# Which engine empties PSUM in three blocks of a weight gradient: the fourth quarter of `gw2`'s fifth to seventh block from VectorE to ScalarE

## The chip, the cores and the metric

The kernel runs on one core of a Trainium2 chip. Its time is the device time of one execution, in microseconds (us); the figure for a kernel is the median over its runs. A core has a matrix engine (TensorE, PE in the profile; its weight loads are PEld), a vector engine (VectorE, DVE), a scalar engine (ScalarE, ACT), GpSimd (POOL) and SyncE (SP). Each works through its own queue of instructions in order. In this kernel POOL and SP mainly start DMA transfers.

## The reference

Forward and backward pass of two residual blocks with layer norm in front, on one sequence of 2048 x 448 in bfloat16: a spectral filter (2-D real FFT, product with learned complex weights, inverse FFT), then an MLP over the sequence axis with 1792 hidden units.

```python
x = A_x
h  = x + irfft2(rfft2(layernorm(x)) * (w_r + 1j * w_i))
u  = gelu(einsum("bsd,sf->bdf", layernorm(h), w1) + b1)
h2 = h + transpose(einsum("bdf,fs->bds", u, w2) + b2)
# returned: h2, and the gradients of <h2, grad_out> to
# A_x, w_r, w_i, w1, b1, w2, b2
```

The gradient of `w2` (1792 x 2048, output 6) is the product of the hidden activations with `grad_out`, summed over the 448 channels. The gradient of `w1` (2048 x 1792, output 4) is built in the same way from the normed `h` and the gradient at the hidden units.

## The kernel before

The FFT is done as matmuls with tables: a 16-point part over the rows of a tile, a 128-point part and a 448-point part. `fft_rows`, `fft_cols` and `cmul` are the forward transform and the complex product; `ifft_cols` and `ifft_rows` the inverse. All of it is run twice, once forward and once for the gradient. The program is written in the order of the lines, but a scheduler places the instructions of independent parts between each other, engine by engine, by costs that it assumes; what comes out is a fixed order in each engine's queue. A tile pool gives out buffers in that order as they come free.

The change lies in the last third. There these pieces run side by side:

- `gw2(j, on)` (L657) makes block j of 14 of the gradient of `w2`, 128 rows by 2048. A block is made in four quarters of 512 columns. Each quarter is four matmuls (L662) that add up in one PSUM tile `ps_mm`, and one copy to the bfloat16 tile `s6` in SBUF. The letter `on[n]` says which engine copies quarter n: "a" ScalarE (L194), "v" VectorE (L196). When all four quarters are copied, POOL issues the store of the block (L172). Blocks count from 0; block 0 is called ahead of the transform, blocks 1 to 13 behind it in the text (L697), and the scheduler spreads them over the transform's work.
- `fft_cols` and `cmul` for the gradient: ScalarE copies `gi` (L346) and `ds` (L324), VectorE makes `gg` (L349) and the products (L362 to L365) on which the inverse waits.
- `ifft_cols` (L379, L380): matmuls; ScalarE copies `t1` (L396), VectorE adds and subtracts into `ab2` (L398, L400), and for two tiles the two engines copy one kind each to `ab2` (L194, L196).
- `ifft_rows`, once for each of 16 rows h: two matmuls L409 and two L411 that read `ab2`, ScalarE's copy `eo` (L194), then four matmuls L415 to L418 that read `eo`. Then `norm_back`: ScalarE's `v` (L612), VectorE's L615, L617 and L618, and the store of `gx`.
- the gradient of `w1` (L726 on): 16 blocks of four quarters (the fourth 256 wide), L732, all copied by ScalarE; in between `grad_w` (L712), whose load of `xs_b` needs the buffer that held `goT`.

PSUM has eight banks here in two pools: three buffers `ps_mm` (tag "mm"), which the quarters of `gw2` and of the `w1` gradient share, and five `ps_sp` (tag "sp") for the transform. `s6` has four buffers (tag "w4").

Of the kernel before, what the change touches and what calls it, by code (L numbers as in the profile page):

```python
# [113 lines left out]
def kernel(  # L114
# [32 lines left out]
    def w4(shape, name):  # L147
        return ring.tile(shape, BF16, tag="w4", bufs=4, name=name)
# [13 lines left out]
    def ps_mm(shape, dtype=F32):  # L162
        return psum.tile(shape, dtype, tag="mm", bufs=3, name="ps_mm")
# [7 lines left out]
    def st(out, in_, eng=None):  # L171
        return (eng or po).dma_start(out=out, in_=in_)  # L172
# [19 lines left out]
    def ev(out, in_, on):  # L192
        if on == "a":
            ac.copy(out=out, in_=in_)  # L194
        else:
            ve.tensor_copy(out=out, in_=in_)  # L196
# [460 lines left out]
    def gw2(j, on):  # L657
        s6 = w4([P, S], "s6")
        for n in range(4):
            pw = ps_mm([P, 512])  # L660
            for c in range(4):
                mm = pe.matmul(pw[:], lhsT=g_t[:, c, j * P:(j + 1) * P], rhs=goT[:, c, 512 * n:512 * n + 512],  # L662
                               start=(c == 0), stop=(c == 3))
            ev(s6[:, 512 * n:512 * n + 512], pw[:], on[n])
        first.append(mm)
        return st(out_6[j * P:(j + 1) * P, :], s6[:])
# [28 lines left out]
    st(out_7.rearrange("(q h) -> q h", h=NT), gb2b[:])  # L695

    for j in range(1, NFB):  # L697
        s6_st = gw2(j, "aaav")
        if j == 8:
            s6_mid = s6_st  # L700

# [69 lines left out]
```

## Time and profile before

| what | us |
|---|---|
| median of 3 runs (lowest, highest) | 372.22 (370.95, 372.51) |
| profiled execution | 371.55 |
| its span in the trace | 369.8 |
| TensorE busy in the span | 346.6 |
| VectorE busy | 236.3 |
| ScalarE busy | 217.4 |
| copies of `ps_mm` to `s` on ScalarE (L194) | 107, 57.5 busy |
| copies of `ps_mm` to `s` on VectorE (L196) | 13, 0.69 each |
| TensorE stopped for ScalarE's copies of `ps_mm`, 232 to 369 | 1.5 in 3 waits |

Busy time is the sum of the instructions' lengths in the trace. A matmul's length has the pipeline's fill in it, so two that follow each other without a gap start 0.216 us apart although each is 0.38 long; the text counts from start to start. A few matmul records are missing from a trace, so a group that is printed as x3 can be four. "Idle before" in a row is time in which the engine stood still ahead of the first of the group, with the instruction that ended it.

### The profile page before, as it was taken

What the parts mean: (1) busy time and instruction counts of PE and PEld (TensorE: products, weight loads), DVE (VectorE), ACT (ScalarE), POOL (GpSimd) and SP (SyncE); (2) the same over time, 40 slices, a digit from 0 to 9 for tenths busy, and PEclk for the clock granted to TensorE, in tenths of its full rate; (3) what the DMA queues carried; (4) which work ended last, traced back from release to release, by engine and by line L of the source; (5) the groups of instructions that cost most, each with busy time, mean ns of one, the idle gap of its engine ahead of it and who ended that gap; (6) DMA issues with size and microseconds to landing.
All of it is one profiled execution on the core that took longest, in us unless ns stands there. A gap on an engine that the chain in (4) does not pass through costs nothing.

```text
span 369.8 us, 5755 instructions
## 1 busy us (share of the span) xinstructions
PE 346.6 (94%) x2100; PEld 200.4 (54%) x2115; DVE 236.3 (64%) x557; ACT 217.4 (59%) x415; POOL 61.2 (17%) x107
## 2 busy tenths in 40 slices
PE   0698999999989999999999999999999999999996
PEld 0355667666645555555555555566655555665553
DVE  4873679967744999621167778468996566599000
ACT  2776555446659998109222234967656666777664
POOL 1000000001112211500540000101012522255311
PEclk9999999999999999999999999999999999999999
DMA  7999998997889999999998875791874444956633
GB/s 279 258 257 307 270 274 245 310 240 259 249 251 176 338 346 291 380 401 215 261 224 159 185 147 208 162 182 61 204 199 184 163 177 166 337 187 255 250 150 149
DMA packets 132524, 86.48 MB, mean 234 GB/s; under 512 B 91952, under 2 KB 123824, under 8 KB 131984
## 3 DMA queue, kind: packets, MB, share of 16 engines
q1 hardware_dynamic: 124304, 55.78, 61.2%
q0 software_dynamic: 8048, 30.31, 22.3%
q8 instruction: 16, 0.26, 0.3%
q14 instruction: 12, 0.10, 0.1%
q10 hardware_dynamic: 144, 0.03, 0.0%
HBM read 32.81 MB, written 30.76 MB: 172 GB/s over the span
## 4 chain that ended last, share of the span: by engine, by line
PE 65%; DVE 17%; ACT 8%; DMA 4%; SPq 3%; issue 2%; ACTq 0%; DVEq 0%
PE ps_mm L732 12%; PE ps_mm L662 10%; PE ps_sp L587 7%; PE ps_mm L438 6%; PE ps_mm L519 6%; PE ps_sp L519 5%; PE ps_mm L587 4%; DMA w2T<-in_B_w_dram 4%; DVE junk L615 3%; DVE junk L617 3%; ACT v L610 3%; SPq L175 2%; DVE t_r L362 2%; DVE gg L349 2%; DVE t_i L363 2%
## 5 line engine op out<-in xcount | busy, mean ns | idle before, releaser
L194 ACT CAST s<-ps_mm 128x512 bf16<-128x512 f32 (+1 forms) x107 | 57.5, 557 | 25.6 <-PE ps_mm L662 11.1
L662 PE MATMUL ps_mm<-goT,g_t 128*128 128x512 bf16 x214 | 53.3, 379 | 2.0 <-ACT s L194 1.5
L438 PE MATMUL ps_mm<-go_nat,w2T 128*128 128x448 bf16 x224 | 50.5, 357 | 1.0 <-DMA w2T<-in_B_w_dram 1.0
L732 PE MATMUL ps_mm<-du_t,hlnT 128*128 128x512 bf16 (+1 forms) x251 | 49.3, 352 | 0.3
L643 PE MATMUL ps_mm<-du,w1T 128*128 128x449 bf16 x224 | 43.4, 353 | 0.0
L732 PEld LDWEIGHTS <-hlnT 128*128 128x128 bf16 x256 | 25.1, 98 | 22.2
L587 PE MATMUL ps_sp<-gT,w2c 128*128 128x448 bf16 x140 | 35.6, 352 | 0.0
L610 ACT ACTIVATE v<-ps_mm,nm,rstd_h 128x448 f32<-128x448 f32 x16 | 11.6, 723 | 39.2 <-DVE nm L608 39.2
L172 POOL DMA_DIRECT2D out_dram<-s x29 | 15.6, 539 | 112.4 <-ACT s L194 86.3
L519 PEld LDWEIGHTS <-w1c 128*128 128x128 bf16 x224 | 21.8, 98 | 20.7 <-issue 1.9
L587 PEld LDWEIGHTS <-w2c 128*128 128x128 bf16 x224 | 21.9, 98 | 20.5
L643 PEld LDWEIGHTS <-w1T 128*128 128x128 bf16 x224 | 21.7, 97 | 20.7
L662 PEld LDWEIGHTS <-g_t 128*128 128x128 bf16 x224 | 21.6, 97 | 20.7 <-issue 1.4
L438 PEld LDWEIGHTS <-w2T 128*128 128x128 bf16 x224 | 21.9, 99 | 16.2 <-DMA w2T<-in_B_w_dram 1.9
L349 DVE TENSOR_TENSOR gg<-ps_sp,gi 128x450 bf16<-128x450 f32 x28 | 16.2, 621 | 17.0 <-ACT gi L346 17.0
L587 PE MATMUL ps_mm<-gT,w2c 128*128 128x448 bf16 x84 | 25.0, 352 | 0.0
L519 PE MATMUL ps_mm<-hln,w1c 128*128 128x448 bf16 x112 | 24.4, 352 | 0.5 <-DVE b1col L508 0.2
L194 ACT CAST eo<-ps_sp 128x450 bf16<-128x450 f32 x32 | 17.2, 538 | 12.5 <-PE ps_sp L411 12.2
L519 PE MATMUL ps_sp<-hln,w1c 128*128 128x448 bf16 x112 | 23.1, 352 | 0.0
L311 PE MATMUL ps_sp<-kf,eo 128*128 128x128 bf16 x128 | 9.3, 231 | 14.0 <-DVE eo L305 14.0
L592 DVE SCALAR_TENSOR_TENSOR h<-ps_sp,b2col,hr 128x448 bf16<-128x448 f32 x10 | 6.3, 679 | 25.1 <-PE ps_sp L587 25.1
L615 DVE CUSTOM_DVE_ANT_0 junk<-ps_sp,xr,rneg_x 128x448 bf16<-128x448 f32 x16 | 10.9, 683 | 16.3 <-ACT v L612 16.3
(146 smaller groups left out, 625.9 us busy)
## 6 DMA issues: line engine op xcount, KB each, us to landing
w1c<-in_B_w_dram SPq DMA_DIRECT2D x7, 1024.0 KB, 7.4
w2c<-in_B_w_dram SPq DMA_DIRECT2D x8, 896.0 KB, 12.6
out_dram<-s POOLq DMA_DIRECT2D x14, 512.0 KB, 2.9
out_dram<-s POOLq DMA_DIRECT2D x15, 448.0 KB, 2.9
xs_d<-xs SPq DMA_DIRECT2D x1, 1800.0 KB, 7.7
xs_b<-xs_d SPq DMA_DIRECT2D x1, 1800.0 KB, 8.9
x<-in_A_x_dram SPq DMA_DIRECT2D x4, 448.0 KB, 4.3
go_nat<-in_grad_out_dram SPq DMA_DIRECT2D x2, 896.0 KB, 7.5
```

The lines of the kernel that those rows point to most:

```text
L172: return (eng or po).dma_start(out=out, in_=in_)
L194: ac.copy(out=out, in_=in_)
L349: ve.tensor_tensor(out=gg[:], in0=pr[:], in1=gi[:], op=op)
L438: pe.matmul(pg[:], lhsT=w2T[j][:, t, :], rhs=go_nat[:, t, :], start=(t == 0), stop=(t == NT - 1))
L519: pe.matmul(pu[:], lhsT=wc[:, h, o:o + P], rhs=hln[:, h, :], start=(h == 0), stop=(h == NT - 1))
L587: pe.matmul(p2[i][:], lhsT=w2c[t0 // 4][:, j, i * P:(i + 1) * P], rhs=gT[:, j, :], start=(j == 0), stop=(j == NFB - 1))
L610: ac.activation(out=v[:], in_=ps[:, 0:D], func=ACT.Identity, scale=rstd_c, bias=nm1[:])
L615: ve.tensor_tensor_reduce(out=junk[:], in0=ps[:, 0:D], in1=xhat, scale=rneg_c, scalar=0.0, op0=ALU.mult, op1=ALU.add, accum_out=nm2[:])
L617: ve.scalar_tensor_tensor(out=junk[:], in0=xhat, scalar=nm2[:], in1=v[:], op0=ALU.mult, op1=ALU.add)
L643: w1_last = pe.matmul(pd[:], lhsT=w1T[:, j, :], rhs=du[:, j, 0:D + 1], start=(j == 0), stop=(j == NFB - 1))
L662: mm = pe.matmul(pw[:], lhsT=g_t[:, c, j * P:(j + 1) * P], rhs=goT[:, c, 512 * n:512 * n + 512], start=(c == 0), stop=(c == 3))
L732: pe.matmul(pw[:, 0:wdt], lhsT=hlnT[:, c, h * P:(h + 1) * P], rhs=du_t[:, c, 512 * n:512 * n + wdt], start=(c == 0), stop=(c == 3))
```

## The change

The call of `gw2` for blocks 4, 5 and 6 gets the string "aaaa" in place of "aaav". ScalarE copies the fourth quarter of these three blocks, VectorE no longer does. All other blocks keep "aaav". Nothing of the arithmetic is changed.

```diff
     for j in range(1, NFB):
-        s6_st = gw2(j, "aaav")
+        s6_st = gw2(j, "aaaa" if 4 <= j <= 6 else "aaav")
         if j == 8:
             s6_mid = s6_st
```

The scheduler's order changes with it. On ScalarE the copy of block 4's fourth quarter stands right behind that of the third quarter, ahead of two L324 copies; block 5's stands between the two `ab2` copies; block 6's behind the first row's `eo`. On TensorE the order is the same up to the first quarters of block 6. There, ahead of the first L415, six more matmuls of `gw2` are placed, and every later row of `ifft_rows` has the blocks of `gw2` and of the `w1` gradient six matmuls further on. On VectorE three copies are gone and the later copies of a fourth quarter move by a place or two against L617 and L618. On POOL the store of block 4 stands ahead of the first three loads of `xr` instead of behind them, and some later stores change places with the stores of `gx`. SP's order is the same.

## The prediction

> **What bounds the kernel now.** I read the page's busy shares and chain of waits first. TensorE is busy 94% and holds 65% of the chain, so a microsecond is won only where TensorE stands still. Then I read the windows over the stretch where `gw2` runs beside the inverse transform.
>
> ```profile
> PE 346.6 (94%) x2100; PEld 200.4 (54%) x2115; DVE 236.3 (64%) x557; ACT 217.4 (59%) x415; POOL 61.2 (17%) x107
> PE 65%; DVE 17%; ACT 8%; DMA 4%; SPq 3%; issue 2%; ACTq 0%; DVEq 0%
> ...
> 262.50:274.50 12.00, 11.64 (x86) 8.33 (x86) 12.00 (x23) 7.11 (x14) 1.63 (x3) 1.00 1.06 239
> 274.50:280.10 5.60, 4.20 (x26) 2.35 (x26) 4.05 (x8) 2.81 (x6) 1.08 (x2) 1.00 0.24 97
> 280.10:334.40 54.30, 53.68 (x315) 31.06 (x319) 37.43 (x81) 38.24 (x72) 19.32 (x34) 1.00 0.58 212
> 334.40:369.80 35.40, 31.80 (x168) 16.47 (x169) 7.34 (x16) 22.19 (x44) 10.19 (x19) 1.00 0.51 196
> ```
>
> The columns are window, length, then busy us (and instructions) of TensorE, its weight loads, VectorE, ScalarE, GpSimd. VectorE is full from 262.5 to 274.5 (12.00 of 12.00) while ScalarE works 7.11. From 274.5 to 280.1 TensorE loses 1.40 of 5.60; later it loses little, and the clock is 1.00 throughout. The timeline of TensorE, VectorE and ScalarE in that hole:
>
> ```profile
> 274.73 0.81 PE L662 MATMUL ps_mm<-goT,g_t 128*128 128x512 bf16 x3
> 276.21 0.81 PE L662 MATMUL ps_mm<-goT,g_t 128*128 128x512 bf16 x3 [0.67 <-ACT s L194]
> 276.86 0.36 PE L409 MATMUL ps_sp<-di,ab 128*128 128x225 bf16 x2
> 277.06 0.38 PE L662 MATMUL ps_mm<-goT,g_t 128*128 128x512 bf16 x1
> 278.11 0.38 PE L662 MATMUL ps_mm<-goT,g_t 128*128 128x512 bf16 x1 [0.67 <-ACT s L194]
> ...
> 280.08 2.97 PE L662 MATMUL ps_mm<-goT,g_t 128*128 128x512 bf16 x13
> 283.08 0.26 PE L415 MATMUL ps_sp<-eo,kinv 128*128 128x225 bf16 x1
> ...
> 276.60 0.76 DVE L196 CAST ab<-ps_sp 128x256 bf16<-128x256 f32 x2
> 277.26 1.29 DVE L196 CAST s<-ps_mm 128x512 bf16<-128x512 f32 x2
> ...
> 261.91 0.59 ACT L194 CAST s<-ps_mm 128x512 bf16<-128x512 f32 x1
> 263.51 1.13 ACT L324 CAST ds<-ps_sp 128x450 bf16<-128x450 f32 x2 [1.01 <-PE ps_sp L323]
> 275.58 0.58 ACT L194 CAST s<-ps_mm 128x512 bf16<-128x512 f32 x1 [0.49 <-PE ps_mm L662]
> 277.47 0.59 ACT L194 CAST s<-ps_mm 128x512 bf16<-128x512 f32 x1 [1.31 <-PE ps_mm L662]
> 278.71 0.54 ACT L194 CAST eo<-ps_sp 128x450 bf16<-128x450 f32 x1 [0.66 <-PE ps_sp L411]
> 282.49 0.54 ACT L194 CAST eo<-ps_sp 128x450 bf16<-128x450 f32 x1
> ```
>
> Call the quarter tiles by block and quarter: j4q4 is the fourth of the fifth block. The VectorE row at 277.26 is j4q4 and j5q4 together. The matmuls of j4q4 were over by 262.7 and those of j5q4 by 274.1, so two of the three `ps_mm` buffers sit full, behind VectorE's complex products and `ab` work. Blocks j6q1, q2 and q3 then share the one buffer that ScalarE empties: TensorE stops until the copy of j6q1 (275.58 to 276.16) and again until that of j6q2 (277.47 to 278.06).
>
> **The change, part by part.** *Removed:* three VectorE copies of 128x512, each 0.69 (0.60 from start to start), two at 277.26 and one at 281.21. Alone that is worth nothing, since VectorE's next work waits for ScalarE's `v` anyway. *Added:* the same three copies on ScalarE, 0.58 long and 0.48 from start to start.
>
> j4q4. Its matmuls end about 262.5 (the seven that start at 261.24, four of them its own), and a ScalarE copy starts 0.2 after the last matmul's slot (277.06 + 0.22 + 0.2 = 277.47, the row above), so it runs 262.7 to 263.3. That is inside the 1.01 of idle before 263.51. Queued behind it are the two L324 copies at 263.51, for which the full VectorE waits; they keep 0.2 of slack. Cost 0; without that cover it would be up to 0.58, on VectorE first.
>
> j5q4. It now stands between the two `ab` copies of 274.06 and 274.72: 274.43 to 274.95. The second `ab` copy ends about 275.3 instead of 275.1, before the copy of 275.58, and VectorE reaches the same tile only at 276.98. Cost 0.
>
> j6q4. It stands behind an `eo` copy in the queue, below.
>
> *Moved.* With the buffers free the order of the built program has TensorE doing six more matmuls of `gw2` before the first L415, and all later rows shift by six. POOL's queue gets the store of block j4 ahead of its three `xr` loads instead of behind. The store can issue at 263.3 and takes about 0.54, and POOL's first `xr` load goes at 267.25 because of TensorE and VectorE; cost 0. If it slipped, the first L615 (280.61) would still be more than 4 us behind the third `xr` load's landing (about 270.4 + 5.4). SP's queue is the same.
>
> *The hole.* A 512-wide matmul takes 0.216 from start to start (the 13 at 280.08: 2.97 less one length of 0.38, over 12). In the trace the next matmul could start at 275.38 and starts at 276.21, then 277.28 and 278.11: 2 x 0.83 = 1.67 lost (the printed 0.67 counts from the modelled end). In the changed order, from 275.38: j6q2 to 276.24; two of j6q3 to 276.67 (its buffer is j5q4's, empty at 275.0); the two L409 to 276.87 (`ab`'s first kind is done at 276.1); two of j6q3 to 277.30; three of j6q4 to 277.95 (buffer of j6q1, empty at 276.16); the two L411 to 278.15 (`ab` is done at 277.36); one of j6q4 and two of j7q1 to 278.79. `eo` follows L411's start by 0.39 (278.32 to 278.71) and L415 follows `eo` by 0.59 (278.71 to 279.30), so L415 starts at 277.95 + 0.98 = 278.92, against 279.30. That is 0.38 earlier with six matmuls more behind it, 0.38 + 6 x 0.216 = 1.67: all of the hole.
>
> *The rows.* From there on each row h is one L415 to L418, L409 and L411 (0.79, from 279.30 to 280.08) and then n matmuls of 512, while ScalarE empties quarters and then copies `eo`. L415 waits for `eo`: from the last matmul of the quarter emptied just ahead of it, 0.2 + 0.48 + 0.59 = 1.27. If k matmuls are queued after that quarter, the row loses 1.27 - 0.216k: 0.19 for k = 5, nothing for k = 6. The trace agrees: 280.08 + 13 x 0.216 = 282.88, and L415 comes at 283.08, `eo` at 282.49. Counting k in both orders: before, k is 5 in rows 1, 3, 4 and 8 (4 x 0.19), two rows of `grad w1` lose 0.25 each where a 256-wide quarter stands ahead, and one 0.03: 1.3. After, k is 5 in rows 1, 5, 9, 14 and 15 and row 12 loses 0.05: 1.0. Gain 0.3. Counted through, the last L415 starts at 278.92 + 15 x 0.79 + 179 x 0.216 + 2.2 (five sets of four 256-wide matmuls) + 1.0 = 332.5 against 334.02 in the trace, with two matmuls more behind it: 1.5 + 0.4 = 1.9. (The same count on the old order gives 334.0.)
>
> Behind the last row there are only matmuls back to back (31.80 busy of 35.40, the rest the tail), and ScalarE's 22.19 fits beside them, so the 1.9 arrives at the end. What VectorE is late with, the `grad_w` products that wait for `xs_b`, moves along: its load goes when the last `gw2` matmul has read `goT`, here about 311.1 instead of 312.9.
>
> [...]
>
> **Sum.** 1.67 + 0.3, or 1.9 by the count through. The profiled execution takes 371.55 (span 369.8 and 1.75 around it), so 369.65; the median shown is 372.22, 0.67 above it, so 370.3.
>
> **Rivals.** *More is won (gain 3.0).* If no row waited for `eo` after the shift, the 1.0 left goes too: 372.22 - 3.0 = 369.2. For it: k = 5 misses by only 0.19. Against: five rows have that k.
>
> *The hole becomes a wait for `ab` (gain 1.5).* L411 needs VectorE's last `ab` piece. The trace has it done at 277.36, 0.58 ahead, but a view of waits puts 1.0 of the weight loads' idling at L411 down to VectorE's copies at 277.26. If L411 cannot start before 278.32, as now, 0.38 is given back: 370.7.
>
> *Slower: ScalarE becomes the pacer of the rows.* Its queue is strict, `v` and two or three copies stand ahead of each `eo`, and the shift could leave one copy more there than I count: 0.48 in each of 15 rows, 7.2 - 1.9 = 5.3, so 377.5. It decides from 0.13 a row (the gain is gone) and from 0.25 a row it is slower by more than the line. For it: a row with three copies ahead already loses 0.25 (317.86). Against: ScalarE is busy 38.24 of 54.30, and the formula fits all rows of before within 0.05.
>
> **How the numbers follow.** The line between change and none is 0.5%, 1.86 us. Forecast 0.60, own range 369.8 to 370.8; its middle lies just past the line (370.36), and since VectorE's freed 1.8 is counted at nothing I put 0.36 of it past and 0.24 short. More won 0.12, faster. `ab` 0.10, same. ScalarE as pacer 0.18, of which 0.14 slower and 0.04 same. So faster 0.48, same 0.38, slower 0.14. The bounds of the unknown costs are row waits of nothing (369.2) and of 0.13 a row (372.2); with the spread of the runs, 369.0 to 372.5.
>
> **What would show it.** Right: no TensorE gap ended by a ScalarE copy between 274 and 279, first L415 near 278.9 after six more matmuls, the last near 332.5, and a ScalarE copy near 262.7 with L324 still at 263.5. Wrong: L324 later than 263.6, L411 waiting for VectorE, or rows whose L415 comes over 0.2 after the last matmul's slot.

## The result and the profile after

The changed kernel takes 370.37 us, the median of 13 runs (369.15 to 371.92); the kernel before, run beside it, takes 371.81 (13 runs, 370.95 to 373.69). The ratio is 0.9954 with a 95% interval of 0.9937 to 0.9971, so the change takes off 1.7 us (1.1 to 2.3); the two medians alone differ by 1.44. An unchanged time (a ratio of 1) lies outside the interval, the 0.5% line inside it. The profiled execution takes 369.54 and its span is 367.8, against 371.55 and 369.8.

This execution starts the first matmul of the gradient's inverse transform (L379) at 263.77, the one of before at 263.91. I therefore compare distances from that instruction. From it to the first L415 the kernel before needs 15.39 us and the changed one 15.03, with six more matmuls done in between; to the end of the span 105.89 and 104.03, which is 1.86 less. The span is printed to 0.1, so a distance to the end is good to some 0.05.

The page's busy shares and chain of waits, and the same four windows as before, with their ends moved to where this execution's stages end (length, then busy us and instructions of TensorE, weight loads, VectorE, ScalarE, GpSimd, then the clock, the DMA share and GB/s):

```profile
PE 347.4 (94%) x2115; PEld 200.6 (55%) x2115; DVE 234.6 (64%) x554; ACT 218.8 (60%) x418; POOL 61.2 (17%) x107
PE 67%; DVE 18%; ACT 8%; DMA 4%; issue 2%; ACTq 0%; DVEq 0%
...
262.50:274.50 12.00, 11.86 (x88) 8.35 (x86) 12.00 (x23) 7.91 (x15) 2.15 (x4) 1.00 1.19 240
274.50:280.10 5.60, 5.60 (x34) 3.10 (x32) 2.71 (x6) 3.97 (x8) 1.09 (x2) 1.00 0.95 231
280.10:332.90 52.80, 52.55 (x315) 30.49 (x314) 37.45 (x81) 38.08 (x72) 18.79 (x33) 1.00 0.57 207
332.90:367.80 34.90, 31.45 (x168) 16.17 (x166) 6.72 (x15) 21.79 (x43) 10.19 (x19) 1.00 0.50 194
```

The second window is the hole. TensorE is busy 5.60 of 5.60 there, where it was 4.20. VectorE lost three copies (557 instructions to 554) and is as full as before in the first window, 12.00 of 12.00; ScalarE got three (415 to 418). The timeline of TensorE, ScalarE and VectorE in the same stretch:

```profile
274.38 2.32 PE L662 MATMUL ps_mm<-goT,g_t 128*128 128x512 bf16 x10
276.54 0.36 PE L409 MATMUL ps_sp<-di,ab 128*128 128x225 bf16 x2
276.74 1.24 PE L662 MATMUL ps_mm<-goT,g_t 128*128 128x512 bf16 x5
277.82 0.36 PE L411 MATMUL ps_sp<-di,ab 128*128 128x225 bf16 x2
278.02 0.81 PE L662 MATMUL ps_mm<-goT,g_t 128*128 128x512 bf16 x3
278.80 0.26 PE L415 MATMUL ps_sp<-eo,kinv 128*128 128x225 bf16 x1
...
279.58 2.54 PE L662 MATMUL ps_mm<-goT,g_t 128*128 128x512 bf16 x11
282.15 0.26 PE L415 MATMUL ps_sp<-eo,kinv 128*128 128x225 bf16 x1
...
262.60 0.59 ACT L194 CAST s<-ps_mm 128x512 bf16<-128x512 f32 x1 [0.23 <-PE ps_mm L662]
263.37 1.14 ACT L324 CAST ds<-ps_sp 128x450 bf16<-128x450 f32 x2 [0.19 <-PE ps_sp L323]
...
274.19 0.59 ACT L194 CAST s<-ps_mm 128x512 bf16<-128x512 f32 x1
278.21 0.54 ACT L194 CAST eo<-ps_sp 128x450 bf16<-128x450 f32 x1 [0.26 <-PE ps_sp L411]
...
276.46 0.76 DVE L196 CAST ab<-ps_sp 128x256 bf16<-128x256 f32 x2
```

Neither of the two rows that ended in "[0.67 <-ACT s L194]" is left: ten matmuls run on without a stop, and the groups between L409, L411 and L415 follow at once. The two copies that freed the buffers are ScalarE's rows at 262.60 (fifth block) and 274.19 (sixth block). The first fills idle time: L324 has 0.19 of idle ahead of it where it had 1.01, and still starts when its own input comes. The view of what TensorE waited for, in the last third, has the `ps_mm` copies of ScalarE at 0.2 in one wait, after 1.5 in three.

### The profile page after: what moved, and what is told of

It reads as the page before. It is cut to its first block, busy times and chain, and to the rows that moved or that the text cites. A ratio compares the mean times of both kernels' runs of the same rounds, so it can differ in the third digit from the quotient of the medians.

```text
span 367.8 us, 5768 instructions
## 1 busy us (share of the span) xinstructions
PE 347.4 (94%) x2115; PEld 200.6 (55%) x2115; DVE 234.6 (64%) x554; ACT 218.8 (60%) x418; POOL 61.2 (17%) x107
## 4 chain that ended last, share of the span: by engine, by line
PE 67%; DVE 18%; ACT 8%; DMA 4%; issue 2%; ACTq 0%; DVEq 0%
PE ps_mm L732 12%; PE ps_mm L662 10%; PE ps_sp L587 7%; PE ps_mm L438 7%; PE ps_mm L519 6%; PE ps_sp L519 5%; PE ps_mm L587 4%; DVE junk L615 3%; DVE junk L617 3%; ACT v L610 3%; DMA w2T<-in_B_w_dram 3%; DVE t_r L362 2%; DVE gg L349 2%; DVE t_i L363 2%; PE ps_sp L321 2%
## 5 line engine op out<-in xcount | busy, mean ns | idle before, releaser
L194 ACT CAST s<-ps_mm 128x512 bf16<-128x512 f32 x110 | 59.5, 559 | 23.8 <-PE ps_mm L662 8.0
L662 PE MATMUL ps_mm<-goT,g_t 128*128 128x512 bf16 x224 | 54.8, 379 | 0.2 <-ACT s L194 0.2
L194 ACT CAST eo<-ps_sp 128x450 bf16<-128x450 f32 x32 | 17.2, 537 | 12.4 <-PE ps_sp L411 12.2
L615 DVE CUSTOM_DVE_ANT_0 junk<-ps_sp,xr,rneg_x 128x448 bf16<-128x448 f32 x16 | 10.9, 682 | 16.3 <-ACT v L612 16.3
```

What stands on the lines that cost most here:

```text
L615: ve.tensor_tensor_reduce(out=junk[:], in0=ps[:, 0:D], in1=xhat, scale=rneg_c, scalar=0.0, op0=ALU.mult, op1=ALU.add, accum_out=nm2[:])
```

## The experiments

All were compared with the kernel before on the same chip: its median was 372.14 (31 runs) beside the four kernels `e_block4`, `e_block5`, `e_block6` and `e_block4up`, and 372.24 (32 runs) beside the other four. "To the end" is the distance from the first L379 of the gradient to the end of the span: 105.89 before, 104.03 with the change.

### The fifth block's copy alone (e_block4)

```diff
-        s6_st = gw2(j, "aaav")
+        s6_st = gw2(j, "aaaa" if j == 4 else "aaav")
```

> Only block 4's fourth quarter on ScalarE. Buffers (my theory): one of the two stuck ps_mm buffers is enough to close the hole, since two buffers in turn keep TensorE fed (j6q3 reuses j6q1's, empty 0.1 us before it is wanted). TensorE's order is that of the full change, so the span falls by the full 1.9 us, no TensorE gap between 274.5 and 280. Rival, relief of VectorE or count of copies moved: a third of it, 0.6 us.

370.27 (8 runs), ratio 0.9943 (0.9923 to 0.9963). First L415 after 15.03, to the end 104.04: both are those of the whole change, within 0.01. TensorE and VectorE in the timeline:

```profile
275.98 2.32 PE L662 MATMUL ps_mm<-goT,g_t 128*128 128x512 bf16 x10
278.13 0.36 PE L409 MATMUL ps_sp<-di,ab 128*128 128x225 bf16 x2
...
278.06 0.74 DVE L196 CAST ab<-ps_sp 128x256 bf16<-128x256 f32 x2
278.73 0.67 DVE L196 CAST s<-ps_mm 128x512 bf16<-128x512 f32 x1
```

The sixth block's quarter is still held until VectorE's copy at 278.73. TensorE does its ten matmuls all the same, ending 0.6 before that copy starts, with the two buffers that are left.

### The sixth block's copy alone (e_block5)

```diff
+        s6_st = gw2(j, "aaaa" if j == 5 else "aaav")
```

> Only block 5's fourth quarter on ScalarE. Buffers: the same full 1.9 us, by the other stuck buffer. Rival, relief of VectorE: 0.6 us. If each copy had a share of its own, blocks 4 and 5 alone would add up to the whole; by my theory each alone is the whole.

369.98 (12 runs), ratio 0.9947 (0.9927 to 0.9966); first L415 after 15.03, to the end 103.99. Now it is the fifth block's quarter that stays behind VectorE, to 280.77, and again the stops are gone (TensorE and VectorE in the timeline):

```profile
278.02 2.32 PE L662 MATMUL ps_mm<-goT,g_t 128*128 128x512 bf16 x10
...
280.77 0.68 DVE L196 CAST s<-ps_mm 128x512 bf16<-128x512 f32 x1
```

The gains of the parts do not add: each of the two copies brings all of it alone. One buffer more is enough, and it does not matter which.

### The seventh block's copy alone (e_block6)

```diff
+        s6_st = gw2(j, "aaaa" if j == 6 else "aaav")
```

> Only block 6's fourth quarter on ScalarE. Buffers: both buffers stay stuck, TensorE keeps both stops of 0.83 us between 275 and 279, and the rows lose 1.15 against 1.3 us: gain 0.1 us, no change. Rival, relief of VectorE: 0.6 us faster.

371.88 (12 runs), ratio 0.9987 (0.9969 to 1.0005); first L415 after 15.39 as before, to the end 105.76, 0.13 less. TensorE's stops stay where they were:

```profile
276.35 0.81 PE L662 MATMUL ps_mm<-goT,g_t 128*128 128x512 bf16 x3 [0.67 <-ACT s L194]
276.99 0.36 PE L409 MATMUL ps_sp<-di,ab 128*128 128x225 bf16 x2
277.19 0.38 PE L662 MATMUL ps_mm<-goT,g_t 128*128 128x512 bf16 x1
278.24 0.38 PE L662 MATMUL ps_mm<-goT,g_t 128*128 128x512 bf16 x1 [0.67 <-ACT s L194]
```

This copy comes after the hole, and taking it from VectorE is worth next to nothing. So the third part of the change does not matter.

### Half of each held copy taken from VectorE, the buffers still held (e_split)

```diff
-            ev(s6[:, 512 * n:512 * n + 512], pw[:], on[n])
+            if j in (4, 5) and n == 3:
+                ev(s6[:, 1536:1792], pw[:, 0:256], "v")
+                ev(s6[:, 1792:2048], pw[:, 256:512], "a")
+            else:
+                ev(s6[:, 512 * n:512 * n + 512], pw[:], on[n])
```

> The fourth quarter of blocks 4 and 5 is halved: VectorE copies columns 0 to 255, ScalarE 256 to 511. VectorE is relieved by half and ScalarE takes over half, but both ps_mm buffers are still held until VectorE comes to its half behind the ab work. Buffers: TensorE keeps both stops between 275 and 279 (first matmul of the inverse to first L415 15.4 us, as before), gain at most 0.3 us, from the rows. Rival, relief of VectorE: about a third of the full gain or more, 0.6 us, with the stops shorter.

372.03 (12 runs), ratio 0.9993 (0.9969 to 1.0018); first L415 after 15.39, to the end 105.85. VectorE's two copies at the end of its backlog shrank from one row of 1.29 to this one of 0.76:

```profile
277.03 0.76 DVE L196 CAST ab<-ps_sp 128x256 bf16<-128x256 f32 x2
277.69 0.76 DVE L196 CAST s<-ps_mm 128x256 bf16<-128x256 f32 x2
```

TensorE nevertheless stops for 0.67 twice (until 276.65 and until 278.55). Both stops end with ScalarE's copy of the quarter before (276.02 and 277.91), as in the kernel before. So neither split tile was free for it: their halves start at 277.69 on VectorE and at 279.58 on ScalarE. Less work for VectorE, with the buffers held at least as long, is worth nothing. In the built order ScalarE's halves stand even later, behind `eo` (279.15), so this is a test of VectorE's load and not of splitting a tile at its best.

### Two more quarters behind VectorE (e_two_more_held)

```diff
+        s6_st = gw2(j, "aavv" if 4 <= j <= 5 else "aaav")
```

> Blocks 4 and 5 give their third quarter to VectorE too (aavv). Buffers: block 4 alone now holds two of three buffers from 262 to 277, so TensorE can place 15 matmuls of gw2 fewer ahead of the first L415 (93 against 108): 3.2 us of idle, of which 0.9 comes back because L415 starts earlier and 0.3 to 0.6 in the rows; about 1.8 us slower than before. Rival, engine time: VectorE has 1.2 us more behind its ab work, where it waits for v for 2.1 us anyway, so no change.

375.46 (7 runs), ratio 1.0082 (1.0054 to 1.0111): 3.0 more, where 1.8 was expected; to the end 109.52, 3.63 more. TensorE's rows:

```profile
276.42 0.36 PE L409 MATMUL ps_sp<-di,ab 128*128 128x225 bf16 x2 [1.21 <-DVE ab L398]
277.59 0.37 PE L411 MATMUL ps_sp<-di,ab 128*128 128x225 bf16 x2 [0.81 <-DVE ab L196]
278.18 0.38 PE L662 MATMUL ps_mm<-goT,g_t 128*128 128x512 bf16 x1 [0.22 <-DVE s L196]
...
279.79 4.21 PE L662 MATMUL ps_mm<-goT,g_t 128*128 128x512 bf16 x13
283.83 0.26 PE L415 MATMUL ps_sp<-eo,kinv 128*128 128x225 bf16 x1
```

With the buffers held by VectorE, TensorE has nothing left to do but the transform and waits for VectorE itself. The thirteen matmuls at 279.79 took 4.21; in the kernel before thirteen took 2.97. The windows of this kernel say why; the third figure from the end is the granted clock:

```profile
276.00:278.70 2.70, 1.23 (x7) 0.56 (x8) 2.70 (x7) 0.53 (x1) 0.00 (x0) 1.00 0.00 0
278.70:279.70 1.00, 1.00 (x8) 0.85 (x7) 0.62 (x2) 0.37 (x1) 0.41 (x1) 0.59 0.08 16
279.70:280.70 1.00, 1.00 (x5) 0.41 (x4) 0.69 (x2) 0.26 (x1) 0.13 (x1) 0.50 0.29 119
280.70:281.70 1.00, 1.00 (x4) 0.39 (x3) 0.39 (x1) 0.00 (x0) 0.00 (x0) 0.50 0.97 377
281.70:282.70 1.00, 1.00 (x4) 0.35 (x3) 0.96 (x3) 0.00 (x0) 0.13 (x1) 0.71 0.07 25
282.70:283.70 1.00, 1.00 (x7) 0.47 (x5) 0.32 (x1) 0.96 (x3) 0.80 (x2) 1.00 0.06 25
```

With the mixed windows (0.59 and 0.71) split between 0.50 and 1.00, the clock is at half for an estimated 0.82 + 1 + 1 + 0.58 = 3.4 us. The first row of the inverse transform, L415 to L415, therefore took 5.25, where a row of thirteen matmuls without a wait takes 3.59 in the kernel before: 1.66 more. Without it the loss to the end is 3.63 - 1.66 = 1.97, near the 1.8 that the buffers were expected to cost. The runs agree: six of the seven executions have a mean granted clock of 0.995, and the one with 1.000 took 374.27, which is 2.0 above the median of before.

### Every later fourth quarter on ScalarE too (e_block4up)

```diff
+        s6_st = gw2(j, "aaaa" if j >= 4 else "aaav")
```

> All four quarters on ScalarE for every block from 4 to 13. Theory: the hole is closed (1.67 us), but in the rows three copies in a line stand ahead of most eo copies and nearly every row waits 0.19 us for eo: rows lose 2.6 us where the full change loses 1.1 by the same count, so 1.5 us slower than the full change and 0.4 us faster than before. Rival, the fewer copies VectorE has the better: at least as fast as the full change, 1.9 us or more faster than before.

371.62 (12 runs), ratio 0.9992 (0.9975 to 1.001). First L415 after 15.02, so the hole is closed as well; to the end 105.41, which is 1.4 more than with the change; the interval of its ratio lies just above that of the change. TensorE and ScalarE in two of the rows:

```profile
284.94 2.75 PE L662 MATMUL ps_mm<-goT,g_t 128*128 128x512 bf16 x12
287.73 0.26 PE L415 MATMUL ps_sp<-eo,kinv 128*128 128x225 bf16 x1
288.51 2.75 PE L662 MATMUL ps_mm<-goT,g_t 128*128 128x512 bf16 x12
291.29 0.26 PE L415 MATMUL ps_sp<-eo,kinv 128*128 128x225 bf16 x1
...
286.65 0.58 ACT L194 CAST s<-ps_mm 128x512 bf16<-128x512 f32 x1 [0.28 <-PE ps_mm L662]
287.13 0.54 ACT L194 CAST eo<-ps_sp 128x450 bf16<-128x450 f32 x1
```

Twelve matmuls are 12 x 0.216 = 2.59, but L415 comes 287.73 - 284.94 = 2.79 after the first of them. From L415 to L415 it is 0.79 + 2.59 + 0.19 = 3.57, the formula with k = 5, and the trace has 3.56 and 3.57 in row after row. Here a ScalarE copy stands close ahead of every `eo`. So the same move that frees a buffer has a price where it lands among the rows. This is the place of the rival in which ScalarE paces the rows, at 0.19 a row and not at 0.48.

### Seeking a better order (e_second_quarter, e_eo_vector)

The first keeps only the sixth block's copy and, for the blocks that run among the rows, gives VectorE the second quarter instead of the fourth, so that another number of matmuls stands behind the quarter emptied ahead of `eo`.

```diff
+        s6_st = gw2(j, "aaaa" if j == 5 else "avaa" if j > 6 else "aaav")
```

> Block 5 all on ScalarE, blocks 7 to 13 give VectorE the second quarter in place of the fourth (avaa). By the count of the rows they lose 0.9 instead of 1.1 us; 0.2 us faster than the full change, 2.1 faster than before. Rival: the place of VectorE's quarter in the block matters more, since its buffer is held in the middle of a block: TensorE stops for ps_mm and the gain shrinks.

369.89 (12 runs), ratio 0.9939 (0.9917 to 0.9961); to the end 103.85, 0.18 less than with the change, where 0.2 was expected; in the trace the rows wait 0.90 for `eo` in all, after 1.06. It is the lowest ratio of the set. Its interval overlaps that of the change, so only the trace speaks for a lead over it, and one trace of each is little for 0.18.

The second moves the `eo` copy of the first eleven rows to VectorE and all fourth quarters from the fifth block on to ScalarE.

```diff
-        ev(eo[:], pq[:], "a")
+        ev(eo[:], pq[:], on)
...
-        py = ifft_rows(ab2, di1, h)
+        py = ifft_rows(ab2, di1, h, "v" if h < 11 else "a")
...
+        s6_st = gw2(j, "aaaa" if j > 3 else "aaav")
```

> Blocks 4 to 13 all on ScalarE, and the eo copy of rows 0 to 10 on VectorE instead. The row's wait for eo no longer stands behind quarters in ScalarE's queue. If VectorE has eo done in time (its row: eo 0.6, L615 0.6, L617 0.7, L618 0.4, started by v), rows 1 to 10 lose nothing: 0.8 us faster than the full change, 2.7 faster than before. Rival: eo then stands behind L618 of the row ahead on VectorE, some 2.9 + 0.6 = 3.5 us after the last L415, and rows of 3.6 us lose up to 0.2 each as now.

370.59 (12 runs), ratio 0.9955 (0.9925 to 0.9985); to the end 104.68, 0.65 more than with the change, where 0.8 less was expected; the rival that stood beside that expectation came true. VectorE and TensorE in one row:

```profile
280.34 0.69 DVE L615 CUSTOM_DVE_ANT_0 junk<-ps_sp,xr,rneg_x 128x448 bf16<-128x448 f32 x1 [1.36 <-ACT v L612]
281.78 0.39 DVE L618 TENSOR_TENSOR gx<-junk,go_r 128x448 bf16<-128x448 bf16 x1
282.09 0.62 DVE L196 CAST eo<-ps_sp 128x450 bf16<-128x450 f32 x1
284.07 0.68 DVE L615 CUSTOM_DVE_ANT_0 junk<-ps_sp,xr,rneg_x 128x448 bf16<-128x448 f32 x1 [1.36 <-ACT v L612]
...
282.76 0.26 PE L415 MATMUL ps_sp<-eo,kinv 128*128 128x225 bf16 x1
283.55 2.97 PE L662 MATMUL ps_mm<-goT,g_t 128*128 128x512 bf16 x13
286.50 0.26 PE L415 MATMUL ps_sp<-eo,kinv 128*128 128x225 bf16 x1
```

The wait for `eo` did not go away; it stands in row after row. VectorE stands idle 1.36 for `v`, then does L615, L617 and L618 and only then `eo`, so each row goes round through L415, `v`, VectorE's three steps and `eo`: 286.50 - 282.76 = 3.74, of which the work of TensorE is 0.79 + 13 x 0.216 = 3.60. The other 0.14 is lost in every such row.

## Why the prediction held

This execution reaches the first L379 of the gradient 0.14 before the one that the prediction was read from. The times in this section have 0.14 added, so that they stand beside the prediction's.

- *What bounds the kernel: two of three `ps_mm` buffers held behind VectorE.* Shown from both sides. Letting go of either one, at either end of the backlog, closes the hole (`e_block4`, `e_block5`); half the work taken off VectorE with the buffers still held closes nothing (`e_split`); two more held opens it wider (`e_two_more_held`). The prediction used both freed buffers in its walk through the order and did not see that one suffices. In each run that closed the hole TensorE's order changed together with the buffers; how much of the gain an unchanged order would bring was not measured.
- *The hole, 1.67.* 15.39 to 15.03 is 0.36, and six more matmuls are 6 x 0.216 = 1.30: 1.66. First L415 278.80 + 0.14 = 278.94, foretold 278.92. L411 at 277.96, foretold 277.95, against 278.32 before.
- *The copies at no cost.* The fifth block's started at 262.74 (262.7 foretold) and L324 at 263.51, unmoved. The sixth's started at 274.33 (274.43). Three copies more on ScalarE cost nothing that the trace shows, and a fourth quarter of every block from the fifth on does cost, 1.4 us in `e_block4up`. Which engine was idle at that place decided: from 262.5 to 274.5 of the kernel before, VectorE worked 12.00 of 12.00 and ScalarE 7.11.
- *The rows, 0.3.* Waits of 1.06 in all are left (three of 0.19, two of 0.23, one of 0.03), where 1.0 was foretold and 1.3 stood before; the gain here is 0.2. One of 0.19 is in the timeline above: eleven matmuls from 279.58, in that view's clock, are 2.38, and L415 comes 2.57 after the first. The two of 0.23 lie just past the 0.2 that the prediction had set as a sign of being wrong; two rows of before already stood at 0.25. The last L415 starts at 332.59, foretold 332.5 (the terms as printed add up to 332.6). The later rows do not all stand six matmuls further on, as the part on the change and the prediction have it: counted by weight loads the lead is six at the first L415, between one and six at the later ones, and two at the last, which is what the count through used.
- *The sum, 1.9.* 1.86 in the trace, 1.7 (1.1 to 2.3) in the runs. The median, 370.37, is 0.07 above the forecast, and that closeness is in part luck: the forecast was taken from a median of 372.22 over 3 runs, and over 13 runs that of the kernel before is 371.81, from which 1.9 less would be 369.9.
- *What moves along.* The load of `xs_b` was issued at 311.28, foretold 311.1, against 313.13 before (the prediction had 312.9 there). VectorE still waits for it, 1.19 instead of 1.50.
- *More is won*: no; the rows' waits stayed. *The hole becomes a wait for `ab`*: no; L411 runs at 277.96 straight behind the matmuls, 0.6 after `ab` was done (276.60 + 0.76 = 277.36). It does take place in `e_two_more_held`, with 0.81. *ScalarE becomes the pacer*: not with three copies, but with all of them, at 0.19 a row.

The prediction said that the middle of its own range lies just past the 0.5% line, and gave the largest part of its chances, 0.48, to that side. The ratio, 0.9954, falls 0.04% short of the line, and its interval does not tell the two apart.

What was not tried: a fourth `ps_mm` buffer in place of one of the transform's five, and an order in which no row waits for `eo`, which would be worth up to the 1.06 that is left.

## What to carry to other kernels

A full `ps_mm` buffer was held here until its copy's turn came in the queue of the engine that empties it: the matmuls of the fifth block's fourth quarter were over by 262.7, and VectorE copied it at 277.26. So where TensorE stops, look for the buffers that another engine holds, and not only for the copy that ends the wait: the rows here named ScalarE (0.67 twice), and VectorE was the cause. Move the one or two copies that stand in a backlog to the engine that idles there; one buffer set free in three was worth all of the gain (104.04 and 103.99 to the end, against 104.03 with the whole change). Moving every such copy had a price here: 0.19 in row after row where a quarter's copy stood close ahead of `eo` in ScalarE's queue, and 1.4 to the end (`e_block4up`).

## What the runs showed of the hardware

In two traces the granted clock fell to 0.50 after stops of TensorE that were each shorter than the drop that followed. Stops of 1.21, 0.81 and 0.22 us with few matmuls between 275.2 and 278.2 in `e_two_more_held` were followed by 3.4 us at half clock, an estimate from the windows above, and the row behind them took 1.66 more, which the expectation did not have (and one execution of the seven, with a mean clock of 1.000, shows no drop); two stops of 0.83 with 1.07 of matmuls between them, in the kernel before, left it at 1.00. The same drop stands in the profiled execution of `e_block5`, in a part that the change does not touch: TensorE waits 2.32 us for the load of `w2T`, until 77.62 (0.71 in the kernel before and 1.06 with the change, the clock at 1.00 behind both), and the windows behind it read

```profile
78.00:79.00 1.00, 1.00 (x10) 0.84 (x9) 0.59 (x1) 0.20 (x1) 0.00 (x0) 0.90 0.84 181
79.00:80.00 1.00, 1.00 (x4) 0.39 (x3) 0.85 (x3) 0.34 (x1) 0.00 (x0) 0.50 1.36 271
...
82.00:83.00 1.00, 1.00 (x8) 0.66 (x7) 0.37 (x2) 0.19 (x1) 0.00 (x0) 0.90 0.79 221
```

which, split in the same way, is 0.2 + 3 + 0.2 = 3.4 us again. With that wait and drop this execution took 373.23, where the median of the kernel is 369.98: the span of one execution says little of a change of 0.5%, and the distance from a common instruction says it. How long a stop has to be for the clock to fall, and what sets the 3.4 us, no run here shows.
